# Attention in 64x64 array tiles, one block for output and next scores, the state summed in SBUF, and four PSUM banks for the MLP

## The chip, the cores and the metric

One core of one Trainium2 chip runs the program. The metric is the device time of an execution in microseconds (us); smaller is better. A run counts as slow when it is over 1.5% above the fastest of its kernel. Engines: PE is TensorE (PEld its weight loads), DVE is VectorE, ACT is ScalarE, POOL is GpSimd.

## The reference

A causal linear attention (4 batches, 8 heads, 768 positions, head size 64, a decay per head) feeds an MLP over 3072 tokens.

```python
intra = einsum('bhij,bhjd->bhid', einsum('bhic,bhjc->bhij', qb, kb) * Dmask, vb)   # per block of 64 positions
inter = einsum('bhid,bhde->bhie', qb * lam_pow, kv_state)
kv_state = lam_block * kv_state + einsum('bhsd,bhse->bhde', kb_dec, vb)
...
h = x @ w_in                     # x: 3072 x 512, w_in: 512 x 2048
s = sin(alpha * h)
g = h + s * s / (alpha + 1e-9)
out = g @ w_out                  # 2048 x 512
```

## The kernel before

The kernel works in 24 attention steps of 128 positions and in six MLP chunks of 512 tokens. A helper records every instruction, and a list scheduler in the program then fixes one static order for each engine; TensorE's order is the order of recording. Each engine works through its order as it stands, so an instruction that waits holds up those behind it.

An **A-group** is one slice of the first MLP half: four matmuls into one PSUM bank, a sine on ScalarE, a square on GpSimd (some on VectorE or ScalarE), and a **combine** on VectorE, which reads the bank a second time and so gives it back. A **B-group** is four matmuls of an output tile; after the last of four, ScalarE copies the tile out. An attention step is: **preparation** (k and q are scaled, v is cast), transposes of q and k, scores, the **mask** on VectorE (the causal mask times the scores, from PSUM into SBUF), output, and state.

```python
NPS = 5                                     # PSUM banks of the MLP
def next_bank():
    i = nm_at[0] % NPS
    nm_at[0] += 1
    return i

def att_S(s):                               # scores, then the mask
    ...
    for jp in range(HP):
        for h in range(2):
            rows = slice(64 * h, 64 * h + 64)
            last = e.matmul(A_ps[:, 4 * h + jp, :], qkT[j][rows, 4 + jp, :], qkT[j][rows, jp, :])
    ...
    rec("DVE", lambda e: e.tensor_tensor(S_m[j][:, :, :], A_ps[:, :, :], mask_b, ALU.mult), 1.25, ...)

def att_O(s, bank=None):                    # inter + intra, x copy, state in PSUM, two casts on ScalarE
    ...

def grp_A(c, m):
    i = next_bank()
    ...                                     # 4 matmuls -> m_ps[i]; sine on ACT -> t16
    if (c in (0, NCH - 1) and m % 4 == 3) or (c == 1 and m % 8 == 3):
        sq_eng, sq_dur = "DVE", 0.57
    elif c == 1 and m % 8 == 7:
        sq_eng, sq_dur = "ACT", 0.65
    else:
        sq_eng, sq_dur = "POOL", 1.05
    ...                                     # square -> u16; combine on DVE reads u16 and m_ps[i] -> gT

prep_next(4, fast=True)                     # at the end of A0: q of step 4 on DVE (fast), k on POOL
...
for m in range(NM):                         # A1: the first half of chunk 1, with steps 8 to 11
    op = grp_A(1, m)
    if m % 4 == 0:
        prep_next(9 + m // 4, soft=[op])
    attend(8, m, 4, 1, 3, 0)                # scores of the step at m % 4 == 1;
                                            # output, then the next step's transposes, at m % 4 == 3
    if m % 4 == 3:
        prep_v(9 + m // 4, soft=[P.ops[-1]])
```

The transposes write into the same PSUM pair `A_ps` that holds the scores until the mask has read them.

I name the stages by what runs: start (steps 0 to 3), A0 (first half of chunk 0), B0 (second half, with steps 4 to 7), A1 (first half of chunk 1, with steps 8 to 11), the mixed loop (second half of chunk c and first half of chunk c+1, with steps 12 to 23, then without attention), and the tail (second half of the last chunk).

Of the kernel before, what the change touches and what calls it, by code (L numbers as in the profile page):

```python
# [14 lines left out]
class Op:  # L15
    __slots__ = ("eng", "fn", "deps", "dur", "idx", "sem_after", "slot", "kslot",
                 "pos", "users", "start", "end", "nbytes", "clock", "prio", "signal", "soft", "soft_users")

    def __init__(self, eng, fn, dur, idx):
        self.eng, self.fn, self.dur, self.idx = eng, fn, dur, idx  # L20
        self.deps = set()
        self.soft = ()
        self.slot = None
        self.kslot = 0
        self.signal = False
        self.prio = idx


class Program:
# [110 lines left out]
    def emit(self, nc, sem):  # L140
# [9 lines left out]
        for op in order:  # L150
            k = known[op.eng]
            need = {}
            for d in op.deps:
                if d.slot is not None:
                    key, val = ("dma", d.slot), d.kslot
                else:
                    if d.eng == op.eng and op.slot is None and d.eng == "PE":
                        continue
                    key, val = d.eng, d.pos
                if k.get(key, 0) >= val:  # L160
                    continue
                if key not in need or need[key][0] < val:
                    need[key] = (val, d)
# [44 lines left out]
def bass_lightning_attn__then__act_snake_kernel(  # L208
# [24 lines left out]
    NPS = 5  # L233
# [5 lines left out]
    with es:  # L239
# [17 lines left out]
        Zs = ring("Zs", 2, [128, HP, 128], BF16)  # L257
# [26 lines left out]
        Z_ps = es.enter_context(nc.psum_tensor("Z_ps", [128, HP, D], F32))  # L284
# [11 lines left out]
        def next_bank():  # L296
            i = nm_at[0] % NPS
            nm_at[0] += 1
            return i
# [13 lines left out]
        def consts():  # L313
# [26 lines left out]
            for i in range(2):  # L340
                rec("DVE", lambda e, i=i: e.memset(Zs[i][:, :, :], 0.0), 0.3, writes=[f"Zs.{i}"])
# [3 lines left out]
        def alpha_ops():  # L345
            rec("ACT", lambda e: e.dma_start(alpha_r[:, :], moe_alpha.rearrange("(m p) -> m p", p=128)), 0,
                writes=["alpha_r"], slot="alpha", nbytes=8192)
            rec("PE", lambda e: e.transpose(Z_ps[:, 0, 0:NM], alpha_r[:, :], identf[0:NM, 0:NM]), 0.3,
                reads=["alpha_r", "identf"], writes=["Z"])
            rec("ACT", lambda e: e.copy(alpha_sb[:, :], Z_ps[:, 0, 0:NM]), 0.2, reads=["Z"], writes=["alpha"])  # L350
# [17 lines left out]
        def prep(s, fast=False, soft=()):  # L368
            n, r, c = s % NB, s % RL, s % RC
            Lq_b = bass.AP(Lq, n * H, [[NB * H, 128], [1, H], [0, D]])  # L370
            Lk_b = bass.AP(Lk, n * H, [[NB * H, 128], [1, H], [0, D]])
            done = rec("POOL", lambda e: e.tensor_tensor(k2[c][:, :, :], k32[r][:, :, :], Lk_b, ALU.mult), 1.05,
                       reads=[f"k32.{r}", "Lk"], writes=[f"k2.{c}"], soft=soft)
            rec("DVE" if fast else "POOL", lambda e: e.tensor_tensor(q2[c][:, :, :], q32[r][:, :, :], Lq_b, ALU.mult),
# [10 lines left out]
        def att_T(s, bank=None):  # L385
            c, j = s % RC, s % 2
            if bank is None:
                dst = bass.AP(A_ps, 0, [[1024, 128], [1, 512]]).bitcast(BF16).rearrange("p (a b) -> p a b", b=128)
                key = "S0"
# [4 lines left out]
            def pe(e):  # L394
                for jp in range(HP):
                    last = e.transpose(dst[:, jp, :], q2[c][:, 2 * jp:2 * jp + 2, :], ident[:, :])  # L396
                for jp in range(HP):
                    last = e.transpose(dst[:, 4 + jp, :], k2[c][:, 2 * jp:2 * jp + 2, :], ident[:, :])  # L398
                return last
            rec("PE", pe, 0.75, reads=[f"q2.{c}", f"k2.{c}", "ident"], writes=[key])  # L400
            rec("DVE", lambda e: e.tensor_copy(qkT[j][:, :, :], dst), 0.7, reads=[key], writes=[f"qkT.{j}"])  # L401

        def att_S(s):
            j = s % 2

            def pe(e):
                for jp in range(HP):
                    for h in range(2):
                        rows = slice(64 * h, 64 * h + 64)
                        last = e.matmul(A_ps[:, 4 * h + jp, :], qkT[j][rows, 4 + jp, :], qkT[j][rows, jp, :])  # L410
                return last
            rec("PE", pe, 0.6, reads=[f"qkT.{j}"], writes=["S0", "S1"])
            mask_b = bass.AP(mask, 0, [[128, 128], [0, 8], [1, 128]])
            rec("DVE", lambda e: e.tensor_tensor(S_m[j][:, :, :], A_ps[:, :, :], mask_b, ALU.mult), 1.25,  # L414
                reads=["S0", "S1", "mask"], writes=[f"S_m.{j}"])
            last_mask[0] = P.ops[-1]

        def att_O(s, bank=None):
            n, c, j = s % NB, s % RC, s % 2
            if bank is None:  # L420
                dst, key = A_ps[:, 4:8, :], "S1"
            else:
                dst = m_ps[bank][:, :].rearrange("p (a b) -> p a b", b=128)
                key = f"m.{bank}"
            has_state = n > 0

            def pe(e):
                if has_state:
                    for jp in range(HP):
                        e.matmul(dst[:, jp, :], Zs[(s - 1) % 2][:, jp, :], qkT[j][:, jp, :],  # L430
                                 start=(jp == 0), stop=False, skip_group_check=True)
                for jp in range(HP):
                    for h in range(2):
                        last = e.matmul(  # L434
                            dst[64 * h:64 * h + 64, jp, :], v2[c][:, 2 * jp + h, :], S_m[j][:, 4 * h + jp, :],
                            start=(not has_state and jp == 0), stop=(jp == HP - 1), skip_group_check=True)
                return last
            rec("PE", pe, 0.9,
                reads=[f"qkT.{j}", f"v2.{c}", f"S_m.{j}"] + ([f"Zs.{(s - 1) % 2}"] if has_state else []),
                writes=[key])  # L440
            ch, col = s // 4, 128 * (s % 4)
            x = ch % NX
            rec("ACT", lambda e: e.copy(xT[x][:, :, col:col + 128], dst), 0.62, reads=[key],  # L443
                writes=[f"x.{x}.{s % 4}"])
            if n < NB - 1:
                def pz(e):
                    for jp in range(HP):
                        for h in range(2):
                            last = e.matmul(
                                Z_ps[64 * h:64 * h + 64, jp, :], k2[c][:, 2 * jp + h, :], v2[c][:, 2 * jp + h, :],  # L450
                                start=(n == 0 and jp == 0), stop=(n == NB - 2 and jp == HP - 1),
                                skip_group_check=True)
                    return last
                rec("PE", pz, 0.3, reads=[f"k2.{c}", f"v2.{c}"], writes=["Z"])
                for h in range(2):
                    rows, cols = slice(64 * h, 64 * h + 64), slice(64 * h, 64 * h + 64)
                    rec("ACT", lambda e, rows=rows, cols=cols: e.copy(  # L457
                        Zs[j][rows, :, cols], Z_ps[rows, :, :]), 0.4, reads=["Z"], writes=[f"Zs.{j}"])
# [54 lines left out]
        def warm(n):  # L513
            def pe(e):
                for _ in range(n):
                    last = e.matmul(m_ps[2][:, :], ident[:, :], zeros[:, :])
                return last
            rec("PE", pe, 0.3 * n, reads=["ident", "zeros"], writes=["m.2"])
# [9 lines left out]
        W2_A, LD_A, W2_B, LD_B, LD_A1 = (7, 13), (10, 15), (2, 6), (3, 7, 11, 15), (3,)  # L528

# [11 lines left out]
        def attend(base, i, per, at_S, at_O, ahead, fast=False):  # L541
            s = base + i // per
            if s >= NSTEP:
                return
            if i % per == at_S:
                att_S(s)
                if ahead == 1:
                    prep_next(s + 1, fast, soft=[last_mask[0]])
            elif i % per == at_O:
                att_O(s)  # L550
                if ahead == 1:
                    prep_v(s + 1, soft=[P.ops[-1]])
                if s + 1 < NSTEP:
                    att_T(s + 1)
                if ahead == 2:
                    prep_next(s + 2, fast, soft=[last_mask[0]])
                    if s + 2 < NSTEP:
                        prep_v(s + 2, soft=[last_mask[0]])

        prep(0, fast=True)  # L560
        att_T(0, bank=3)
        for s in range(4):
# [5 lines left out]
            att_S(s)  # L568
            warm(2)
            if s < 3:  # L570
                att_T(s + 1, bank=3 if s % 2 else 4)
            warm(1)
            att_O(s, bank=s % 2)
# [12 lines left out]
        banks = [next_bank() for _ in range(4)]  # L586
        for m4 in range(4):
            for s4 in range(4):
                op = grp_B(0, s4, m4, banks[s4])
# [8 lines left out]
                if i in S_B:  # L598
                    s = 4 + S_B.index(i)
                    att_S(s)  # L600
                    prep_next(s + 1, fast=True, soft=[last_mask[0]])
                if i in O_B:
                    s = 4 + O_B.index(i)
                    att_O(s)
                    prep_v(s + 1, soft=[P.ops[-1]])
                    att_T(s + 1)
        for m in range(NM):
# [4 lines left out]
            if m % 4 == 0:  # L612
                prep_next(9 + m // 4, soft=[op])
            attend(8, m, 4, 1, 3, 0)
            if m % 4 == 3:
                prep_v(9 + m // 4, soft=[P.ops[-1]])
        prep_next(13, soft=[last_mask[0]])
        prep_v(13, soft=[last_mask[0]])
        for c in range(1, NCH):
            for i in range(NM):  # L620
                if i % 4 == 0:
                    bank = next_bank()
                grp_B(c, i // 4, i % 4, bank)
                if c + 1 < NCH:
                    attend(4 * (c + 2), 2 * i, 8, 2, 6, 2)
                    grp_A(c + 1, i)
                    attend(4 * (c + 2), 2 * i + 1, 8, 2, 6, 2)
# [34 lines left out]
```

## Time and profile before

The time was 234.58 us (median of 3 runs, 233.88 to 235.54), the profiled span 232.7 us. The stages below run from the first matmul of one to the first of the next.

| stage | start | A0 | B0 | A1 | mixed loop | tail |
|---|---|---|---|---|---|---|
| us | 22.51 | 15.82 | 25.64 | 21.84 | 129.82 | 17.10 |

The first two lines are the page's totals and the granted TensorE clock in 40 slices of the span (tenths, 9 is full).

```profile
PE 211.0 (91%) x1571; PEld 105.4 (45%) x1598; DVE 128.4 (55%) x169; ACT 123.2 (53%) x217; POOL 134.1 (58%) x141
...
PEclk9999999999999999999999999999999999999999
```

TensorE is the bound at 91% and no slice loses its clock. Where it isn't the bound is told by stages. The next view gives busy time of each engine in A0, A1, a stretch of the mixed loop and the tail.

```profile
core 0: us, PE busy (x) PEld busy (x) DVE busy (x) ACT busy (x) POOL busy (x), PEclk, DMA share, GB/s
22.50:38.30 15.80, 14.07 (x63) 6.07 (x65) 12.37 (x17) 11.10 (x18) 12.73 (x13) 1.00 1.18 208
...
64.00:85.80 21.80, 20.16 (x196) 11.03 (x201) 17.38 (x24) 18.00 (x34) 18.71 (x19) 1.00 1.21 236
85.80:187.20 101.40, 100.64 (x772) 50.70 (x783) 56.50 (x72) 58.56 (x103) 69.50 (x69) 1.00 0.41 92
...
215.60:232.70 17.10, 13.98 (x64) 6.17 (x64) 1.92 (x3) 3.03 (x5) 0.29 (x1) 1.00 0.20 77
```

In the mixed loop TensorE is busy 100.64 of 101.40 us, so only less work for TensorE helps there. In A1 all four engines are busy over 17 of 21.8 us: TensorE has hardly any waits, but nobody has much room.

One attention step of the mixed loop, as TensorE's timeline shows it (start, length, what, operation, out<-in, count):

```profile
122.81 0.40 PE L410 MATMUL A_ps<-qkT 64*128 64x128 bf16 x8
...
126.60 0.39 PE L430 MATMUL A_ps<-qkT,Zs 128*128 128x128 bf16 x4
126.92 0.41 PE L434 MATMUL A_ps<-S_m,v_1 128*64 128x128 bf16 x8
127.17 0.29 PE L449 MATMUL Z_ps<-v_1,k_1 128*64 128x64 bf16 x8
127.39 0.40 PE L396 MATMUL A_ps<-ident,q_2 128*128 128x128 bf16 x4
...
131.39 0.40 PE L410 MATMUL A_ps<-qkT 64*128 64x128 bf16 x8
```

From scores to scores a step takes 131.39 - 122.81 = 8.58 us. "64*128" and "128*64" are the shapes in which the array is used; it changes four times per step.

```profile
66.25 1.22 DVE L414 TENSOR_TENSOR S_m<-A_ps,mask 128x1024 bf16<-128x1024 f32 x1 [2.07 <-PE A_ps L410]
```

### The profile page before, as it was taken

How to read it: one execution, taken by the hardware profiler on the slowest of the kernel's cores; microseconds unless marked ns; L12 is line 12 of the kernel's file. 1: busy time of each engine (PE TensorE's matmuls, PEld its weight loads, DVE VectorE, ACT ScalarE, POOL GpSimd, SP SyncE). 2: the span in 40 equal slices, each digit the busy share in tenths (PEclk: the TensorE clock that was granted, in tenths of full speed). 3: DMA queues.
4: the chain of work that ended last, by engine and by line, in shares of the span. 5: the costliest groups of instructions: out<-in, count | busy, mean ns of one | idle time of the engine just before them, and what ended most of it. 6: DMA issues, size and time to landing. Idle time of an engine off the chain costs nothing.

```text
span 232.7 us, 3924 instructions
## 1 busy us (share of the span) xinstructions
PE 211.0 (91%) x1571; PEld 105.4 (45%) x1598; DVE 128.4 (55%) x169; ACT 123.2 (53%) x217; POOL 134.1 (58%) x141
## 2 busy tenths in 40 slices
PE   0687988697999989999999999999999999999994
PEld 0354433244455544455455455455455444444441
DVE  1664599745668876645636645546556535545300
ACT  4345774032787885655655655575465454454221
POOL 3253789340569897669568568758754554454100
PEclk9999999999999999999999999999999999999999
DMA  6999999999999999999670110111011011101112
GB/s 142 219 182 159 206 195 206 216 207 202 250 294 203 226 215 218 249 223 219 139 180 1 48 45 9 40 45 43 5 45 46 2 45 45 45 3 45 64 71 90
DMA packets 82752, 29.61 MB, mean 127 GB/s; under 512 B 75552, under 2 KB 79664, under 8 KB 82736
## 3 DMA queue, kind: packets, MB, share of 16 engines
q1 hardware_dynamic: 74880, 18.88, 42.7%
q0 software_dynamic: 4224, 4.19, 11.4%
q10 hardware_dynamic: 3632, 6.31, 7.4%
q8 instruction: 12, 0.20, 0.4%
q14 instruction: 4, 0.03, 0.0%
HBM read 27.28 MB, written 6.29 MB: 144 GB/s over the span
## 4 chain that ended last, share of the span: by engine, by line
PE 73%; DVE 8%; DMA 5%; SPq 4%; ACT 3%; issue 2%; POOL 2%; ACTq 0%; POOLq 0%
PE m_ps L498 33%; PE m_ps L470 28%; SPq L310 4%; DVE gT L488 3%; DMA w<-in_moe_w_out_dram 3%; PE A_ps L410 3%; DVE S_m L414 3%; PE A_ps L434 2%; DMA q_3<-in_q_dram 2%; PE A_ps L396 2%; PE A_ps L398 1%; POOL u_1 L486 1%; PE A_ps L430 1%; POOL u_0 L486 1%; ACT xT L443 1%
## 5 line engine op out<-in xcount | busy, mean ns | idle before, releaser
L498 PE MATMUL m_ps<-w,gT 128*128 128x512 bf16 x377 | 94.0, 380 | 2.7 <-DVE gT L488 1.3
L470 PE MATMUL m_ps<-xT,w 128*128 128x512 bf16 x366 | 92.3, 380 | 3.8 <-DVE gT L488 1.7
L498 PEld LDWEIGHTS m_ps<-w,gT 128*128 128x128 bf16 x384 | 36.6, 98 | 46.6 <-DVE gT L488 1.7
L470 PEld LDWEIGHTS m_ps<-xT,w 128*128 128x128 bf16 x384 | 35.2, 98 | 43.0 <-DVE gT L488 3.1
L486 POOL TENSOR_TENSOR u_0<-t_0 128x512 bf16<-128x512 bf16 x24 | 25.1, 1047 | 23.1 <-ACT t_0 L474 23.1
L414 DVE TENSOR_TENSOR S_m<-A_ps,mask 128x1024 bf16<-128x1024 f32 x24 | 29.4, 1223 | 11.7 <-PE A_ps L410 11.0
L488 DVE SCALAR_TENSOR_TENSOR gT<-u_1,r_sb,m_ps 128x512 bf16<-128x512 bf16 x24 | 17.9, 746 | 23.3 <-POOL u_1 L486 23.3
L488 DVE SCALAR_TENSOR_TENSOR gT<-u_3,r_sb,m_ps 128x512 bf16<-128x512 bf16 x24 | 17.9, 744 | 20.7 <-POOL u_3 L486 19.9
L486 POOL TENSOR_TENSOR u_1<-t_1 128x512 bf16<-128x512 bf16 x24 | 24.9, 1038 | 5.1 <-ACT t_1 L474 5.0
L486 POOL TENSOR_TENSOR u_2<-t_2 128x512 bf16<-128x512 bf16 x24 | 24.9, 1039 | 5.1 <-ACT t_2 L474 5.0
L474 ACT ACTIVATE t_2<-m_ps,alpha_sb 128x512 bf16<-128x512 f32 x24 | 16.5, 687 | 19.4 <-PE m_ps L470 19.3
L474 ACT ACTIVATE t_1<-m_ps,alpha_sb 128x512 bf16<-128x512 f32 x24 | 16.5, 687 | 18.1 <-PE m_ps L470 18.1
L486 POOL TENSOR_TENSOR u_3<-t_3 128x512 bf16<-128x512 bf16 x12 | 12.5, 1039 | 23.0 <-ACT t_3 L474 23.0
L474 ACT ACTIVATE t_0<-m_ps,alpha_sb 128x512 bf16<-128x512 f32 x24 | 16.5, 687 | 15.3 <-PE m_ps L470 15.2
L488 DVE SCALAR_TENSOR_TENSOR gT<-u_0,r_sb,m_ps 128x512 bf16<-128x512 bf16 x24 | 17.8, 740 | 10.1 <-POOL u_0 L486 10.1
L488 DVE SCALAR_TENSOR_TENSOR gT<-u_2,r_sb,m_ps 128x512 bf16<-128x512 bf16 x24 | 17.9, 744 | 9.6 <-POOL u_2 L486 9.6
L443 ACT CAST xT<-A_ps 128x512 bf16<-128x512 f32 x20 | 11.6, 582 | 20.9 <-PE A_ps L434 15.4
L506 ACT COPY osb<-m_ps 128x512 f32<-128x512 f32 x24 | 14.1, 586 | 15.6 <-PE m_ps L498 15.5
L474 ACT ACTIVATE t_3<-m_ps,alpha_sb 128x512 bf16<-128x512 f32 x24 | 16.5, 687 | 4.0 <-PE m_ps L470 3.8
L401 DVE COPY qkT<-A_ps 128x1024 bf16<-128x1024 bf16 x20 | 13.7, 684 | 4.7 <-PE A_ps L398 4.7
L457 ACT CAST Zs<-Z_ps 64x256 bf16<-64x256 f32 x40 | 14.6, 366 | 0.6
L410 PE MATMUL A_ps<-qkT 64*128 64x128 bf16 x192 | 10.0, 226 | 2.0 <-DVE qkT L401 1.9
(173 smaller groups left out, 176.8 us busy)
## 6 DMA issues: line engine op xcount, KB each, us to landing
out_dram<-osb ACTq DMA_DIRECT2D x24, 256.0 KB, 2.0
w<-in_moe_w_in_dram POOLq DMA_DIRECT2D x4, 512.0 KB, 8.0
w<-in_moe_w_out_dram POOLq DMA_DIRECT2D x4, 512.0 KB, 6.8
k_0<-in_k_dram SPq DMA_DIRECT2D x4, 256.0 KB, 4.4
q_0<-in_q_dram SPq DMA_DIRECT2D x4, 256.0 KB, 5.1
v_0<-in_v_dram SPq DMA_DIRECT2D x4, 256.0 KB, 5.4
k_1<-in_k_dram SPq DMA_DIRECT2D x4, 256.0 KB, 5.5
q_1<-in_q_dram SPq DMA_DIRECT2D x4, 256.0 KB, 5.8
```

The lines of the kernel that those rows point to most:

```text
L310: rec_load(lambda e, a=a, d=dst[r]: e.dma_start(d[:, :, :], a), [f"{nme}32.{r}"], f"{nme}{r}", 330000, after)
L401: rec("DVE", lambda e: e.tensor_copy(qkT[j][:, :, :], dst), 0.7, reads=[key], writes=[f"qkT.{j}"])
L410: last = e.matmul(A_ps[:, 4 * h + jp, :], qkT[j][rows, 4 + jp, :], qkT[j][rows, jp, :])
L414: rec("DVE", lambda e: e.tensor_tensor(S_m[j][:, :, :], A_ps[:, :, :], mask_b, ALU.mult), 1.25, reads=["S0", "S1", "mask"], writes=[f"S_m. ...
L443: rec("ACT", lambda e: e.copy(xT[x][:, :, col:col + 128], dst), 0.62, reads=[key], writes=[f"x.{x}.{s % 4}"])
L457: rec("ACT", lambda e, rows=rows, cols=cols: e.copy(Zs[j][rows, :, cols], Z_ps[rows, :, :]), 0.4, reads=["Z"], writes=[f"Zs.{j}"])
L470: last = e.matmul(m_ps[i][:, :], w1[:, kc, 128 * m:128 * (m + 1)], xT[x][:, kc, :], start=(kc == 0), stop=(kc == NKC - 1))
L474: rec("ACT", lambda e: e.activation(t16[tt][:, :], m_ps[i][:, :], ACTF.Sin, scale=alpha_sb[:, m:m + 1]), 0.7, reads=[f"m.{i}", "alpha"], w ...
L486: return e.tensor_tensor(u16[tt][:, :], t16[tt][:, :], t16[tt][:, :], ALU.mult)
L488: rec("DVE", lambda e: e.scalar_tensor_tensor(out=gT[g][:, m, :], in0=u16[tt][:, :], scalar=r_sb[:, m:m + 1], in1=m_ps[i][:, :], op0=ALU.m ...
L498: last = e.matmul(m_ps[bank][:, :], gT[g][:, m, 128 * s4:128 * (s4 + 1)], w2[:, m, :], start=(m == 0), stop=(m == NM - 1))
L506: rec("ACT", lambda e: e.copy(osb[o][:, :], m_ps[bank][:, :]), 0.6, reads=[f"m.{bank}"], writes=[f"o.{o}"])
```

## The change

The intent is to give TensorE less to do per attention step. All attention products use 64x64 tiles of the array, four of which run at the same time. One block holds the first half of the output of step o, the scores of the next step s, and the second half of the output, so the array changes shape twice instead of four times per step. The state is added up in SBUF by VectorE (`Zacc`) and cast by GpSimd, instead of staying in PSUM and being cast twice by ScalarE. The output now takes a PSUM pair of its own, so the MLP has four banks, and bank 0 of these is kept for B-groups: A-groups rotate over three.

```diff
-    NPS = 5
+    NPS = 4
@@
         def next_bank():
-            i = nm_at[0] % NPS
+            i = 1 + nm_at[0] % (NPS - 1)
@@
-        def att_S(s):
-        def att_O(s, bank=None):
+        def mm_S(e, s, h, ch):
+            r, a, j = h // 4, h % 4, s % 2
+            return e.matmul(A_ps[half(ch), h, :], qkT[j][half(r), 4 + a, half(ch)], qkT[j][half(r), a, :])
+        ...                                              # mm_intra, mm_inter, mm_Z: 64x64 tiles as well
+        def att(o, s):
+            ...
+                fence = rec("PE", first, 0.3, reads=reads, writes=["O"])
+            if s is not None:
+                rec("PE", scores, 0.25, reads=[f"qkT.{s % 2}"], writes=["S"])
+            if o is not None:
+                op = rec("PE", second, 0.3, reads=reads, writes=["O"])
+                op.fence = fence
+            if has_Z:
+                ...  op = rec("DVE", lambda e: e.tensor_tensor(acc, z, acc, ALU.add), 0.4, ...)   # Zacc
+            ...      rec("ACT", lambda e: e.copy(xo, O_ps[:, :, 0:2, :]), 0.62, ..., after=after)
+            ...      rec("POOL", lambda e: e.tensor_copy(Zs[o % 2][:, :, :], Zacc[:, :, :]), 0.35, ...)
+            ...      # then the mask of s on DVE
@@
+        SEC_A1, PREP_A1 = (1, 4, 8, 12, 15), (0, 3, 6, 9, 12)
@@
-                op = grp_B(0, s4, m4, banks[s4])
+                op = grp_B(0, s4, m4, s4)
@@                                                       # A1
-            if m % 4 == 0:
-                prep_next(9 + m // 4, soft=[op])
-            attend(8, m, 4, 1, 3, 0)
-            if m % 4 == 3:
-                prep_v(9 + m // 4, soft=[P.ops[-1]])
-        prep_next(13, soft=[last_mask[0]])
-        prep_v(13, soft=[last_mask[0]])
+            if m in PREP_A1:
+                prep_next(9 + PREP_A1.index(m), soft=[op])
+            if m in PREP_A1:
+                prep_v(9 + PREP_A1.index(m), soft=[op])
+            if m in SEC_A1:
+                s = 8 + SEC_A1.index(m)
+                att(s - 1 if s > 8 else None, s)
+                att_T(s + 1)
@@                                                       # mixed loop
-                grp_B(c, i // 4, i % 4, bank)
+                grp_B(c, i // 4, i % 4, 0)
...                                                      # att at i % 4 == 2, transposes at i % 4 == 3
```

The `fence` makes the second half of the output wait for the end of the first, both on TensorE; between TensorE's other instructions the program leaves such waits out.

## The prediction

> **What bounds it now.** Span 232.7 us, TensorE busy 91%, clock 1.00 (page). By stretches (busy table): start to 22.5 us; A0 (first MLP half of chunk 0) 22.5-38.3; B0 (second half, with attention) to 64.0; A1 to 85.8; the mixed loop to 187.2, where TensorE is busy 100.6 of 101.4 us; chunk 4/5 without attention to 215.6; tail. In the mixed loop the timeline gives 8.58 us per attention step: 32 MLP matmuls at 216 ns (6.91) plus 1.67 for attention. Of that 1.67 about 1.29 is streaming and four times ~95 ns is lost where the array shape changes (149 ns between starts instead of 55; 310 instead of 216). The Trainium skill, "TensorEngine Tiling (Array Packing)", Key Properties, says a mode change drains TensorE; the trace agrees. In A1 POOL is busy 18.7 of 21.8 us.
>
> **Gain, on the critical path.** One 64x64 block holds output and next scores; transposes stay 128x128: two shape changes per step instead of four (-0.19 us). Tile pairs start 4 ns apart now, every 53 ns (N=128) or 27 (N=64); with four tiles I estimate first 0.22, scores 0.21, second 0.30, transposes 0.45, changes 0.19: 1.4 us against 1.67. The fence between the halves is covered by the scores in the loop, exposed (~0.2 us) in start and B0. I subtract ~0.1 us: transposes wait for the mask (1.22 us), now behind the state addition on DVE. Mixed loop: about -2.6 us, one score block of that being moved to A1.
>
> **Cost, also on the critical path.**
> - A-groups rotate over three banks only (bank 0 is kept for B). A bank is held 0.65 + 0.42 (last matmul to sine) + 0.69 sine + 0.08 + 1.04 square + 0.04 + 0.74 combine = 3.65 us, plus ~0.06 to return. Five banks: 0.74 us per group, hidden under 0.865. Three: 1.24. So A0 becomes bank-bound: 19.4 us instead of 15.8, and the q preparation on DVE (1.85 us), inside it, is no longer absorbed: about +5 us. B0's second group waits for A0's last bank (+1 us), but the w_out wait (1.0 us) vanishes.
> - Tail: all four last output tiles use bank 0. Each hand-over costs last matmul to copy 0.42 + 0.06 + copy 0.59 + 0.06 = 1.12 instead of 0.22 us; three times +2.7.
> - A1: POOL gets five preparations and three state copies (~0.5 us): about 21.5 us of work after the first square; +2.2 us.
> - Start: x copy behind the state addition, fence: +0.8 us.
> - ACT loses 40 state copies (14.6 us): free time, no gain.
>
> **Sum.** 0.8 + 5 + 0.5 + 2.2 - 2.6 + 2.7 = +8.6 us. Predicted 243 us, range 235 to 250. Faster by over 2%: 0.08; within 2%: 0.20; slower: 0.72.
>
> **What would show it.** A0's matmul starts in bursts of three groups per ~3.7 us, TensorE waiting for the DVE combine; A0 ≥ 19 us. Mixed period ~8.4 us, two ~95 ns losses per step, four tiles starting within ~12 ns. Three ~0.9 us waits on the output copy in the tail. A1 ~24 us, POOL near full. ACT busy ~-14 us.
>
> **What would make it wrong.** TensorE may not be fed 112 small instructions per block (the trace proves only ~32 ns per instruction over 128); then it is slower still. Four tiles might not run together. Or early losses are absorbed by waits I counted as fixed and attention shrinks below 1.2 us: then it is within 2%.

## More of the kernel before

The waits of TensorE, in total over the span (us, times, longest), are few:

```profile
PE A_ps L410 <- DVE qkT L401: 1.9, 3, 0.8
PE m_ps L470 <- DVE gT L488: 1.7, 2, 1.1
PE m_ps L498 <- DVE gT L488: 1.3, 2, 1.0
```

No wait for the mask before the transposes is among them. In A1 the mask (third line) runs while TensorE does two A-groups:

```profile
65.81 0.40 PE L410 MATMUL A_ps<-qkT 64*128 64x128 bf16 x8
...
68.66 0.40 PE L396 MATMUL A_ps<-ident,q_4 128*128 128x128 bf16 x4
```

## The result, and the profile after

The changed kernel took 256.56 us (median of 4 runs, 256.16 to 257.71) against 235.06 us (233.88 to 235.66) for the kernel before in the same rounds. The ratio is 1.093, with a 95% interval of 1.0885 to 1.0974. Ratios here are the mean time of one kernel's fast runs over the mean of the other's in the same rounds, so not quite the ratio of the medians that I quote.

| stage (us) | start | A0 | B0 | A1 | mixed loop | tail | span |
|---|---|---|---|---|---|---|---|
| before | 22.51 | 15.82 | 25.64 | 21.84 | 129.82 | 17.10 | 232.75 |
| after | 24.04 | 21.55 | 25.40 | 37.04 | 126.55 | 19.76 | 254.34 |
| difference | +1.5 | +5.7 | -0.2 | +15.2 | -3.3 | +2.7 | +21.6 |
| predicted | +0.8 | +5 | +0.5 | +2.2 | -2.6 | +2.7 | +8.6 |

Five of six terms are near, and their errors cancel. A1's error, 15.2 less 2.2, is the 13 us by which the sum was off.

The totals and the clock of the page after; the clock now falls in the slices of A1:

```profile
PE 211.1 (83%) x2193; PEld 103.3 (41%) x2222; DVE 133.0 (52%) x187; ACT 110.2 (43%) x177; POOL 141.8 (56%) x161
...
PEclk9999999999998697999999999999999999999999
```

The busy times by stretch, for A0, A1, the mixed loop with attention and the tail:

```profile
24.00:45.60 21.60, 15.29 (x63) 5.50 (x66) 11.93 (x17) 10.83 (x16) 13.67 (x14) 1.00 0.89 157
...
71.00:108.00 37.00, 24.13 (x324) 12.85 (x328) 21.43 (x30) 17.49 (x29) 24.85 (x27) 0.86 1.10 225
108.00:204.90 96.90, 94.86 (x1050) 48.06 (x1062) 57.13 (x79) 48.82 (x78) 69.01 (x75) 1.00 0.23 64
...
234.50:254.30 19.80, 14.54 (x64) 5.93 (x64) 1.92 (x3) 3.06 (x6) 0.33 (x1) 1.00 0.18 66
```

In A1 no engine is busy more than 24.85 of 37.0 us. No engine's throughput bounds it; the engines wait for each other in turn. TensorE's waits (total, times, longest) say on whom:

```profile
PE A_ps L398 <- DVE S_m L508: 10.0, 5, 4.0
PE m_ps L522 <- DVE gT L540: 8.5, 6, 2.6
...
PE m_ps L550 <- ACT osb L558: 2.1, 3, 0.7
```

The first line is new: the five transposes of A1 wait for the mask. The second is the A-groups' wait for a bank (6 times in A0 and A1), the third the tail. The worst mask wait, on TensorE's timeline:

```profile
77.82 0.39 PE L410 MATMUL A_ps<-qkT 64*64 64x128 bf16 x14
...
82.42 0.61 PE L398 MATMUL A_ps<-ident,q 128*128 128x128 bf16 x4 [3.95 <-DVE S_m L508]
82.82 0.63 PE L400 MATMUL A_ps<-ident,k 128*128 128x128 bf16 x4
83.67 5.28 PE L522 MATMUL m_ps<-xT,w 128*128 128x512 bf16 x15 [0.22 <-issue]
```

and on VectorE's, whose fixed order has a square, the state addition and three combines ahead of the mask:

```profile
78.13 0.79 DVE L538 TENSOR_TENSOR u<-t 128x512 bf16<-128x512 bf16 x1 [1.70 <-ACT t L526]
78.84 0.41 DVE L495 TENSOR_TENSOR Zacc<-O_ps,Zacc 128x256 f32<-128x256 f32 x1
79.18 2.05 DVE L540 SCALAR_TENSOR_TENSOR gT<-u,r_sb,m_ps 128x512 bf16<-128x512 bf16 x3
81.15 1.21 DVE L508 TENSOR_TENSOR S_m<-A_ps,mask 128x1024 bf16<-128x1024 f32 x1
```

ScalarE was late as well: its sines stood behind a v copy that waited 2.93 us for a load. That turned out to matter little for this wait (the run with later v copies below still has 3.69 us of it).

```profile
76.32 0.62 ACT L384 CAST v<-v 128x512 bf16<-128x512 f32 x1 [2.93 <-DMA v<-in_v_dram]
76.84 1.84 ACT L526 ACTIVATE t<-m_ps,alpha_sb 128x512 bf16<-128x512 f32 x3
```

The wait has a second cost. The fifteen matmuls at 83.67 take 5.28 us: at first they start some 428 ns apart instead of 216. Over A1 twelve pairs are so far apart, which lost 2.5 us (sum of their distances less 216 ns each). The Trainium skill, "TensorE: Matmul & The Clock Gate", Part 1: The HAM clock gate, says that the array's clock is halved after an idle window of about 3.4 us and that it takes about as long to come back; the trace agrees here in the halving after a wait of 3.95 us, while the way back took longer, about 5.1 us (from 82.42 to 87.49 us).

In the mixed loop and the tail the prediction's picture is there. From block to block a step now takes 129.68 - 121.33 = 8.35 us instead of 8.58:

```profile
121.33 0.24 PE L414 MATMUL O_ps<-S_m,v 64*64 64x128 bf16 x2
...
129.68 0.24 PE L419 MATMUL O_ps<-qkT,Zs 64*64 64x128 bf16 x2
```

A change of the array's shape costs about 93 ns (309 ns between starts where 216 is usual), and there are two per step, as predicted. The Trainium skill, "TensorEngine Tiling (Array Packing)", Key Properties, says that a mode change drains TensorE; the 93 ns fit that, without showing what they are spent on. In the tail each new output tile waits for the copy of the last:

```profile
238.94 3.63 PE L550 MATMUL m_ps<-w,gT 128*128 128x512 bf16 x16 [0.73 <-ACT osb L558]
243.30 3.63 PE L550 MATMUL m_ps<-w,gT 128*128 128x512 bf16 x16 [0.73 <-ACT osb L558]
247.61 3.63 PE L550 MATMUL m_ps<-w,gT 128*128 128x512 bf16 x16 [0.68 <-ACT osb L558]
```

### The profile page after: what moved, and what is told of

The parts are those of the page before. It is cut to its first block, busy times and chain, and to the rows that moved or that the text cites. A ratio compares the mean times of both kernels' runs of the same rounds, so it can differ in the third digit from the quotient of the medians.

```text
span 254.3 us, 5115 instructions
## 1 busy us (share of the span) xinstructions
PE 211.1 (83%) x2193; PEld 103.3 (41%) x2222; DVE 133.0 (52%) x187; ACT 110.2 (43%) x177; POOL 141.8 (56%) x161
## 4 chain that ended last, share of the span: by engine, by line
PE 62%; DMA 13%; DVE 8%; SPq 6%; ACT 5%; POOL 3%; issue 2%; ACTq 0%
PE m_ps L550 28%; PE m_ps L522 26%; SPq L312 6%; DMA w<-in_moe_w_in_dram 4%; DVE gT L540 4%; DMA v<-in_v_dram 3%; ACT t L526 3%; DMA w<-in_moe_w_out_dram 3%; PE O_ps L414 2%; DVE S_m L508 2%; DMA k<-in_k_dram 2%; PE A_ps L398 2%; DMA q<-in_q_dram 2%; POOL u L538 2%; PE A_ps L410 1%
## 5 line engine op out<-in xcount | busy, mean ns | idle before, releaser
L538 POOL TENSOR_TENSOR u<-t 128x512 bf16<-128x512 bf16 x84 | 86.8, 1041 | 57.2 <-ACT t L526 56.9
L540 DVE SCALAR_TENSOR_TENSOR gT<-u,r_sb,m_ps 128x512 bf16<-128x512 bf16 x96 | 70.4, 744 | 68.4 <-POOL u L538 66.5
L526 ACT ACTIVATE t<-m_ps,alpha_sb 128x512 bf16<-128x512 f32 x96 | 65.7, 687 | 75.8 <-PE m_ps L522 75.6
L374 POOL TENSOR_TENSOR k<-k,Lk 128x512 bf16<-128x512 f32 x24 | 25.3, 1055 | 10.6 <-DMA k<-in_k_dram 7.5
L501 ACT CAST xT<-O_ps 128x512 bf16<-128x512 f32 x24 | 14.0, 585 | 36.1 <-DVE Zacc L495 25.7
L384 ACT CAST v<-v 128x512 bf16<-128x512 f32 x24 | 14.7, 616 | 7.6 <-DMA v<-in_v_dram 7.6
L414 PE MATMUL O_ps<-S_m,v 64*64 64x128 bf16 (+1 forms) x384 | 15.4, 215 | 2.2 <-DVE S_m L508 1.6
L376 POOL TENSOR_TENSOR q<-q,Lq 128x512 bf16<-128x512 f32 x15 | 15.6, 1043 | 0.0
L419 PE MATMUL O_ps<-qkT,Zs 64*64 64x128 bf16 x160 | 14.1, 232 | 0.0
L410 PE MATMUL A_ps<-qkT 64*64 64x128 bf16 x384 | 10.7, 225 | 0.8 <-DVE qkT L403 0.8
L424 PE MATMUL O_ps<-v,k 64*64 64x64 bf16 x320 | 11.0, 196 | 0.0
```

Source lines behind the costliest of these rows:

```text
L374: done = rec("POOL", lambda e: e.tensor_tensor(k_out, k_in, Lk_b, ALU.mult), 1.05, reads=[f"k32.{r}", "Lk"], writes=[f"k2.{c}"], soft=soft)
L376: rec("DVE" if fast else "POOL", lambda e: e.tensor_tensor(q_out, q_in, Lq_b, ALU.mult), 0.6 if fast else 1.05, reads=[f"q32.{r}", "Lq"], ...
L384: rec("ACT", lambda e: e.copy(v2[c][:, :, :], v32[r][:, :, :]), 0.62, reads=[f"v32.{r}"], writes=[f"v2.{c}"], soft=soft)
L414: return e.matmul(O_ps[half(h % 2), g, a, i0:128], v2[c][half(r), h, :], S_m[j][half(r), h, i0:128], start=start, stop=True, skip_group_ch ...
L526: rec("ACT", lambda e: e.activation(t16[tt][:, :], m_ps[i][:, :], ACTF.Sin, scale=alpha_sb[:, m:m + 1]), 0.7, reads=[f"m.{i}", "alpha"], w ...
L538: return e.tensor_tensor(u16[tt][:, :], t16[tt][:, :], t16[tt][:, :], ALU.mult)
```

## The experiments

The theory after the result: A1 lost its time to **order and buffers**, not to load. Transposes that stand directly behind the scores in the same PSUM pair must wait for the mask; the mask stands in VectorE's fixed order behind combines which wait for squares, which wait for sines; and three banks leave TensorE no slack to cover it. The rival is the prediction's own reason, GpSimd's load by the fifth preparation and the state casts. A third suspect is the v copies' place on ScalarE.

All kernels gave correct results. Stage times are from each kernel's profiled run; ratios are to the kernel before in the same rounds. One profile's stage time is not exact: in stages that an edit left as in the changed kernel, the start took 24.0 to 25.7 us, A0 20.5 to 22.0 and A1 37.0 to 37.8. In the rounds of sections 1 and 3 and of two runs of section 4 (both changes in the kernel before; squares on ScalarE), many runs of the kernel before were slow (4 of 7, 5 of 11, 3 of 11), and the record gives the verdict "unclear" there; the ratios that I quote are still those of fast runs alone.

### 1. Single remedies in the changed kernel

**Transposes of A1 into the idle MLP bank 0** (so that they need not wait for the mask):

```diff
-                att_T(s + 1)
+                att_T(s + 1, bank=0 if m < 15 else None)
```

> The changed kernel with one edit: in A1 (the second chunk's first MLP half) the transposes that stand directly behind a score block go to MLP bank 0, which is idle there, instead of to the score banks that the mask still has to read (four of the five times). Theory W (transposes wait for the mask, and everything behind them): the waits of 1.6, 4.1, 2.5 and 1.1 us before the transposes vanish, the clock stays at 1.00 in A1, A1 falls from 37.0 to about 25 us and the time from 256.5 to about 245. Rival L (the copies of v, early in ScalarE's fixed order, wait for loads and hold up the sines): A1 falls by less than 4 us, the waits reappear at the next score or MLP group. Rival B (three MLP banks are too few): nothing, at most 1 us.

Measured: 248.16 us, ratio 1.0571 (1.0497 to 1.0645). A1 fell from 37.04 to 29.90 us (-7.1). The waits for the mask went from 10.0 to 1.6 us, and waits for combines, that is for banks, rose from 8.5 to 10.7. The order of the transposes is worth about half of A1's loss, and what it uncovers is the banks.

**v copies of A1 later** (behind the blocks instead of with the preparation):

```diff
-            if m in PREP_A1:
-                prep_v(9 + PREP_A1.index(m), soft=[op])
+            if m in V_A1:                                # (3, 7, 11, 14, 15)
+                prep_v(9 + V_A1.index(m), soft=[op])
```

> The changed kernel with one edit: in A1 the copies of v are recorded 3 to 4 MLP groups later, each still before the output block that needs it. Theory L: the 2.9 us wait of ScalarE for the load of v vanishes, with it the 4.1 us wait of TensorE and the throttled clock; A1 falls from 37.0 to about 27, the time to about 247. Theory W: the waits of the transposes for the mask stay, at 1.5 to 2.5 us each, five times; the 4.1 us one shrinks to that and the clock stays up; A1 falls by 3 to 5 us, time about 252. Theory B: nothing.

Measured: 254.14 us, ratio 1.0838 (1.0716 to 1.0959). A1 fell by 2.0 us to 35.07. The waits for the mask stayed (10.6 us, the longest 3.7). So the load that held up ScalarE is not the main cause: it made the longest wait 0.26 us longer. VectorE's order makes nearly all of it. In this run the state addition (0.42 us, which needs the end of the block), three combines (2.05) and the mask (1.22) follow each other without a gap from 78.68 to 82.21 us, which is 3.53 of the 3.69 us that the transposes wait:

```profile
78.68 0.42 DVE L495 TENSOR_TENSOR Zacc<-O_ps,Zacc 128x256 f32<-128x256 f32 x1 [0.52 <-PE O_ps L424]
79.02 2.05 DVE L540 SCALAR_TENSOR_TENSOR gT<-u,r_sb,m_ps 128x512 bf16<-128x512 bf16 x3
80.99 1.22 DVE L508 TENSOR_TENSOR S_m<-A_ps,mask 128x1024 bf16<-128x1024 f32 x1
```

**Four banks instead of three in A0 and A1** (bank 0 included, as B-groups don't need it then):

```diff
-            i = 1 + nm_at[0] % (NPS - 1)
+            i = nm_at[0] % NPS if chunk[0] < 2 else 1 + nm_at[0] % (NPS - 1)
```

> The changed kernel with one edit: in A0 and A1 the MLP groups rotate over all four MLP banks instead of three (bank 0 is idle there). All theories, for A0: 3.7 us hold over four banks is 0.93 us per group, so A0 falls from 21.6 to about 17 us. For A1: theory B says that it falls by 8 us or more (time about 243); theories W and L say by less than 2 us (time about 251).

Measured: 251.4 us, ratio 1.0699 (1.0571 to 1.0828). A0 fell by 2.8 us to 18.72, A1 by 5.6 to 31.40, between the two readings (8 or more; under 2); B0 gave 1.7 back. The mask waits stayed at 8.6 us.

**Tail over four banks**:

```diff
-                grp_B(c, i // 4, i % 4, 0)
+                grp_B(c, i // 4, i % 4, 0 if c + 1 < NCH else i // 4)
```

> The changed kernel with one edit: the four last output tiles of chunk 5 use banks 0 to 3 instead of all bank 0. The three waits of 0.9 us on the output copy vanish: 2.7 us less, about 253.8 us. Were the tail limited elsewhere (gelu-like combine of the last group, output DMA), the gain would be under 1 us.

Measured: 254.14 us, ratio 1.0825 (1.0718 to 1.0931). The tail fell from 19.76 to 17.10 us, exactly the tail of before. This is the term of the prediction that was right in cause and size.

### 2. Remedies together

**A1 put in order**: transposes two A-groups behind the scores (the last ones, of step 13, in the mixed loop), v copies late, four banks in A1.

```diff
-        SEC_A1, PREP_A1 = (1, 4, 8, 12, 15), (0, 3, 6, 9, 12)
+        SEC_A1, T_A1, PREP_A1 = (0, 4, 8, 12, 15), (2, 6, 10, 14), (0, 3, 6, 9, 12)
@@
                 att(s - 1 if s > 8 else None, s)
-                att_T(s + 1)
+            if m in T_A1:
+                att_T(9 + T_A1.index(m))
...                      # v copies and banks as above; att_T(13) in the mixed loop
```

> The changed kernel with A1 alone edited, three edits together: transposes two MLP groups behind the scores that they overwrite (the last of them in the mixed loop), copies of v later, and four MLP banks in A1. If the order in A1 and its banks are the whole of its loss: no wait of TensorE for the mask over 0.7 us in A1, clock 1.00, A1 from 37.0 to about 24 us, time about 244. Rival (GpSimd's own load, five preparations and three state copies beside twelve squares, bounds A1): GpSimd busy over 90% of A1 and A1 no shorter than 28 us, time about 248.

Measured: 244.09 us median; ratio of the fast runs 1.0362 (1.0299 to 1.0424). The profiled run was odd: 1200.95 us, with every matmul some 1280 ns from the next at a recorded clock of 1.0. It counts as slow, I have no explanation for it, and its profile is not used. The three timed runs were 243.06 to 244.31.

**A0 over five banks** (the four and one half of the output pair, which is idle in A0):

```diff
+            i = nm_at[0] % 5 if chunk[0] == 0 else 1 + nm_at[0] % (NPS - 1)
+            ps = m_ps[i][:, :] if i < NPS else bass.AP(O_ps, 0, [[1024, 128], [1, 512]])
...                      # the sine and the combine read ps, too
```

> The changed kernel with A0 alone edited: its MLP groups rotate over five banks as before the change (the four MLP banks and half of the output pair, idle in A0). If three banks are the whole of A0's loss: A0 from 21.6 to 16 to 17 us, time about 252. Rival (the preparation of q on VectorE, or the loads, hold A0 up whatever the banks, as the four-bank run, 18.7 us, might hint): A0 stays near 18.7.

Measured: 256.49 us, ratio 1.088 (1.0806 to 1.0954): nothing to tell from the changed kernel. The profile fell into a slow run (259.38 us), so I read only its order of events. The first ten groups ran without a wait for a bank; then TensorE waited 3.00 us for a combine (the changed kernel has a wait of 2.55 us near there). And my edit had a flaw: the last group of A0 landed on bank 0, which B0's first tile needs, which cost another wait of 3.20 us. The expected gain went into these two waits.

**All remedies**: the last two and the tail's four banks.

> The changed kernel with the edits of A0 (five banks), A1 (later transposes and copies, four banks) and tail (a bank per tile) together. If the three losses are independent and all that there is beside the start: start 24, A0 17, B0 25.5, A1 24, mixed loop with the rest of the MLP 127, tail 17.1, in all a span of 234.6 and a time of about 236.5, within 1% of the kernel before. If they hide each other (a gain in one stage given back in the next, loads that are not there), 240 or more.

Measured: 242.01 us (6 runs), ratio 1.0296 (1.0249 to 1.0342). A1 is 22.33 us: the joint block, the state sum and the preparations are all still there, and 14.7 of the 15.2 us are gone (2.0 of them came back in the mixed loop, which now holds the transposes of step 13 and begins with a wait for a bank). The next view, in the columns of the busy times above, shows what is left in A1:

```profile
71.90:94.23 22.33, 19.45 (x316) 10.72 (x320) 18.66 (x27) 16.01 (x27) 22.00 (x25) 1.00 1.04 227
```

GpSimd is now busy 22.00 of 22.33 us. So the prediction's count of GpSimd's work was a fair floor for A1; it was not what made 37 us of it.

The total is not the 236.5 us that I expected of independent losses, but falls under the other reading, 240 or more. A0 is still 21.48 us, of which 2.63 is the wait that my flaw in the rotation makes. The reason for the other wait, 3.00 us for a combine, stands on VectorE's timeline

```profile
34.42 3.83 DVE L376 TENSOR_TENSOR q<-q,Lq 128x512 bf16<-128x512 f32 x1
38.17 0.73 DVE L543 SCALAR_TENSOR_TENSOR gT<-u,r_sb,m_ps 128x512 bf16<-128x512 bf16 x1
```

and on GpSimd's at the same time:

```profile
33.66 3.04 POOL L541 TENSOR_TENSOR u<-t 128x512 bf16<-128x512 bf16 x3
36.66 1.03 POOL L374 TENSOR_TENSOR k<-k,Lk 128x512 bf16<-128x512 f32 x1
```

The q preparation, which mostly takes 0.63 to 0.70 us on VectorE in these kernels, took 3.83 us. It ended at 38.25, which is 0.56 us after GpSimd's unbroken run of four operations ended at 37.69. In the kernel before, the same operation took 1.85 us and ended at 34.33, 0.57 us after GpSimd's run had ended at 33.76. The Trainium skill, "SBUF — State Buffer", section "SBUF: two separate sides", says that a VectorE operation with two SBUF inputs and a GpSimd operation that reads SBUF exclude each other for a whole instruction. The 3.83 us fit that, though they span several GpSimd instructions (see the last section); and the combine, with one input in PSUM, took 0.73 to 0.75 us throughout A0.

**All remedies, and the x copy ahead of the state addition in step 3 of the start**:

```diff
-            att(s, None)
+            att(s, None, x_first=s == 3)
```

> The same with one more edit: in the last step of the start the output is copied to x before the state is added up, not after. If the state addition on VectorE delays A0's start: 0.4 us less than the run beside it, all of it in the start. If the start is bound by the loads, nothing.

Measured: 241.86 us, ratio 1.028 (1.0237 to 1.0323), against 1.0296 without it. No difference that these runs can tell; the +1.5 us of the start are not explained by this order.

### 3. What was left of A0, and the mirror in the kernel before

**Rotation of A0 begun on the fifth bank**, so that its last group does not land on bank 0:

```diff
-            i = nm_at[0] % 5 if chunk[0] == 0
+            i = (nm_at[0] + 4) % 5 if chunk[0] == 0
```

> The combination of remedies (transposes two groups later, v copies later, four banks in A1, five in A0, tail over four banks), with the only difference that A0's rotation starts at the half of O_ps, so that its last group lands on O_ps and bank 0, which B0's first tile needs, is free earlier. If the 3.0 us gap at the start of B0 was only this artefact, A0 falls from 21.5 to 18.5 us and the total from 242.0 to about 239 (ratio about 1.017). Rival: the gap only moves (the second tile waits for bank 1 or 2, or the combines end as late as before): A0 stays within 0.5 us of 21.5.

Measured: 239.77 us, ratio 1.0198 (1.0147 to 1.0248). A0 18.68 us, as expected; B0's first wait was the flaw of my edit.

**The q preparation of step 4 on GpSimd**, on top of that:

```diff
-        prep_next(4, fast=True)
+        prep_next(4)
```

> As the run before, and step 4's q preparation at the end of A0 is moved from VectorE (where it took 3.83 us, ending 0.6 us after GpSimd's run of back-to-back squares ended) to GpSimd. Theory that VectorE is starved by GpSimd on an operation with two SBUF inputs: no VectorE operation above 1.6 us is left in A0, the 3.4 us gap of TensorE in A0 goes, A0 is 16 to 17.5 us, total 236 to 238 (ratio 1.005 to 1.015). Rival, that A0 is bound by the amount of work on GpSimd: the 1.05 us more on GpSimd makes A0 no shorter than in the run before.

Measured: 237.95 us, ratio 1.0122 (1.0078 to 1.0167). The total was met, A0 was not: it stayed at 19.47 us (1.6 of which its first two groups lost at half clock). The slow operation had only moved. VectorE's next operation with two SBUF inputs, a square, took 3.56 us

```profile
37.73 3.56 DVE L541 TENSOR_TENSOR u<-t 128x512 bf16<-128x512 bf16 x1
```

while GpSimd ran without a gap until 41.00:

```profile
34.98 3.04 POOL L541 TENSOR_TENSOR u<-t 128x512 bf16<-128x512 bf16 x3
37.98 1.03 POOL L374 TENSOR_TENSOR k<-k,Lk 128x512 bf16<-128x512 f32 x1
38.98 2.02 POOL L541 TENSOR_TENSOR u<-t 128x512 bf16<-128x512 bf16 x2
```

The square ended at 41.29. B0 was shorter by 2.8 us, mostly because a 1.5 us wait for a load of w_out, and the half clock of the matmuls soon after it, did not occur in this run; I claim no cause for that.

**The kernel before, with A1's transposes directly behind the scores**:

```diff
             if i % per == at_S:
                 att_S(s)
+                if ahead == 0:
+                    att_T(s + 1)
```

(and no longer behind the output in A1)

> The kernel before, with one thing of the change: in A1 the transposes of the next step stand directly behind the scores, in the same PSUM pair, instead of two MLP groups later. Theory (placement makes waits for the mask): from the trace of before each of four transposes would then wait 1.2 to 1.4 us for the mask (mask 1.22 us, begun when the scores end), so A1 grows by 3 to 5 us from 25.64/21.84 (B0/A1) to A1 25 to 27 us, total about 239 (ratio 1.015 to 1.02); with five banks and no state addition VectorE is less far behind than in the changed kernel, so the 4 us wait does not appear. Rival (GpSimd throughput sets A1, placement is free): A1 stays 21.8 +- 0.5, ratio 1.00.

Measured: 243.27 us, ratio 1.034 (1.027 to 1.041). A1 grew by 4.4 us to 26.28, inside the expected 3 to 5. Each of the four transposes waits 1.41 us, three of them for the mask (its 1.23 us and the way to and from it), the last for a preparation; two of them:

```profile
72.50 0.38 PE L396 MATMUL A_ps<-ident,q 128*128 128x128 bf16 x4 [1.41 <-DVE S_m L414]
79.10 0.38 PE L396 MATMUL A_ps<-ident,q 128*128 128x128 bf16 x4 [1.41 <-DVE S_m L414]
```

The total grew by more, since B0 was 4.9 us longer in the profiled run: a load of w_out landed later (TensorE waited 2.37 us instead of 0.99) and eight matmuls then started 428 ns apart. TensorE's order is the same as before up to A1, so this is not the edit's place to act; I don't count it, and can't say why the load was late.

**The kernel before, with three banks in A0 and A1**:

```diff
-            i = nm_at[0] % NPS
+            i = 1 + nm_at[0] % 3 if n == 3 else nm_at[0] % NPS      # n is 3 in A0 and A1
...                      # B0's tiles on banks 0 to 3, then the rotation starts anew
```

> The kernel before, with its first MLP half rotating over three PSUM banks in A0 and A1 instead of five (all else as before; the mixed loop keeps five). If three banks alone make A0's loss: A0 15.8 to 19.5-21 us, with TensorE waiting for the combine. A1: the bank period 1.24 us per group times 16 is 19.8 us plus attention, so if banks alone explain A1's loss, A1 becomes 30 us or more; if placement is needed too, A1 grows by 2 to 5 us only. Total 242 to 246 in the second case (ratio 1.03 to 1.045).

Measured: 247.83 us, ratio 1.0546 (1.0485 to 1.0607). A0 grew by 7.2 us to 23.03, A1 by 5.6 to 27.46, and the total is above the expected 242 to 246. Banks alone do not make A1's 37 us.

### 4. Both together, and the starved operations

**The kernel before, with both** (edits of the last two):

> The kernel before, with both single changes: A1's transposes directly behind the scores, and three banks for A0 and A1. Alone they lengthened A1 by 4.4 and 5.6 us. If they add, A1 is 31.9 us (21.84 + 4.4 + 5.6); if they feed each other (TensorE idle longer, half clock, VectorE's order), it is 33 us or more; if the one wait hides in the other, 28 to 30. The changed kernel has 37.0. Ratio to before about 1.08 to 1.09.

Measured: 248.87 us, ratio 1.0602 (1.0521 to 1.0684). A1 29.65 us, +7.8 where the parts were +4.4 and +5.6: the waits partly cover each other. The mask starts at once here, so that each wait is again 1.41 us, and no matmul in A1 ran at half clock:

```profile
81.37 0.38 PE L396 MATMUL A_ps<-ident,q 128*128 128x128 bf16 x4 [1.41 <-DVE S_m L414]
88.31 0.38 PE L396 MATMUL A_ps<-ident,q 128*128 128x128 bf16 x4 [1.41 <-DVE S_m L414]
```

**A0's four VectorE squares on ScalarE** (on top of q on GpSimd):

```diff
-            if (c in (0, NCH - 1) and m % 4 == 3) or (c == 1 and m % 8 == 3):
+            if (c == NCH - 1 and m % 4 == 3) or (c == 1 and m % 8 == 3):
                 sq_eng, sq_dur = "DVE", 0.57
-            elif c == 1 and m % 8 == 7:
+            elif (c == 1 and m % 8 == 7) or (c == 0 and m % 4 == 3):
                 sq_eng, sq_dur = "ACT", 0.65
```

> As the last combination (q preparation on GpSimd), and A0's four squares that VectorE did (m % 4 == 3) are on ScalarE. In the last run the long VectorE operation of A0 was no longer the q preparation but a square of 3.56 us, which TensorE then waited 3.0 us for. Theory (every VectorE operation with two SBUF inputs is starved while GpSimd runs back to back): with none left in A0 apart from the combines (one input in PSUM), no VectorE instruction of A0 is over 0.8 us and A0 falls from 19.5 to 15.5 to 16.5 us, total 234 to 235.5 (ratio 0.995 to 1.003). Rival (GpSimd's own queue delays A0): the longest wait of TensorE in A0 stays about 3 us and A0 above 18 us, now ended by GpSimd's squares.

Measured: 237.92 us, ratio 1.0099 (1.002 to 1.0179). A0 fell to 16.34 us, again with 1.6 lost at half clock in its first two groups, and had no wait of TensorE for a combine left. So A0 was held by starved VectorE operations and not by the amount of GpSimd's work, which this run does not reduce. But the total did not fall as expected: the transposes of step 4 now waited 1.73 us for the q preparation on GpSimd, which is about half of what B0 grew by (26.88 us against 23.73).

**The first group of chunk 2 on bank 1**, which A1 gave up longest ago:

```diff
+        nm_at[0] = 0
         for c in range(1, NCH):
```

> As the run before, and the first MLP half of the mixed loop starts its rotation on bank 1, which A1 gave up longest ago, instead of bank 2. The 1.6 us wait for a combine at the first group of chunk 2 should fall by 0.7 to 0.9 us, nothing else should change: total 0.5 to 1 us below the run before, 233.5 to 235 (ratio 0.99 to 1.00): at best level with the kernel before.

Measured: 236.65 us, ratio 1.0052 (0.9997 to 1.0107). The wait fell from 1.58 to 0.83 us and the mixed loop by 0.9 us; the total came out above the expected range. A0 was 14.78 us without the half clock. This is the best version of the change that I found, and it does not beat the kernel before.

**The kernel before, with A0's squares on ScalarE and step 4's q preparation on GpSimd** (edits as above):

> The kernel before, with the four squares of A0 on ScalarE instead of VectorE and step 4's q preparation on GpSimd. In its trace VectorE's squares took up to 1.5 us and the q preparation 1.85 us in A0, and TensorE had waits of 1.15, 0.52 and 1.02 us for combines there and at the start of B0. If they are the same starvation, A0 and the first wait of B0 shorten by 1 to 2 us together and the total by about that (ratio 0.993 to 0.998); if the step-4 transposes then wait for GpSimd instead, nothing is gained (1.00).

Measured: 233.65 us (233.15 to 234.77, 6 fast runs), ratio 0.9938 (0.9886 to 0.999). A0 went from 15.82 to 14.82 us, although the transposes of step 4 wait 1.63 us here too. It has the lowest time, by 0.6%. The same repair is in the last kernel above, which took 236.65 us in the same rounds, so like for like the repaired change is 1.0052 / 0.9938 = 1.011 times the repaired kernel before (a quotient; no interval was recorded for it).

### 5. The rest of A1

**The kernel before, with both, and A1's preparations as in the change** (five, with v copies at once):

```diff
-            if m % 4 == 0:
-                prep_next(9 + m // 4, soft=[op])
+            if m in (0, 3, 6, 9, 12):
+                prep_next(9 + m // 3, soft=[op])
+                prep_v(9 + m // 3, soft=[op])
...                      # the later v copies and step 13's preparation behind A1 are cut
```

> The kernel before with both single changes (29.65 us in A1) and, as a third part of the change, A1's preparations as the changed kernel has them: five instead of four inside A1 (at groups 0, 3, 6, 9, 12), the v copies on ScalarE directly with them. If the preparations and early v copies are what lifts 29.65 to the changed kernel's 37.0, A1 is 35 us or more. If the rest belongs to the state sum and the joint block of output and next scores, which this kernel doesn't have, A1 is 29 to 32 us.

Measured: 253.4 to 254.46 us in three slow runs and 249.4 in the only fast one; no ratio is given. Inconclusive. The profile is of a slow run (A1 33.81 us), and the fast run is within the range of the kernel without this part (248.36 to 251.57 us), so the preparations' cost can't be told.

**The changed kernel, with the fifth preparation moved out of A1** and its transposes into the mixed loop:

```diff
-        SEC_A1, PREP_A1 = (1, 4, 8, 12, 15), (0, 3, 6, 9, 12)
+        SEC_A1, PREP_A1 = (1, 4, 8, 12, 15), (0, 3, 6, 9)
...                      # step 13 is prepared behind A1; att_T(13) in the mixed loop
```

> The changed kernel with only A1's fifth preparation (step 13: k and q on GpSimd, v on ScalarE) moved behind A1 and its transposes into the mixed loop, as the kernel before has them. This tests the prediction's own term, that GpSimd's load by the fifth preparation sets A1's growth: if so A1 falls by 2 to 3 us from 37.0. If the order and the banks set it, A1 falls by 1.1 to 1.9 us at most (the 1.6 us wait of the last transposes and their 0.45 us leave A1, and some comes back in the mixed loop): total 255 to 256 (ratio 1.085 to 1.09).

Measured: 256.5 us, ratio 1.0878 (1.0772 to 1.0984), the time of the changed kernel. A1 fell by 1.6 us to 35.40 and the mixed loop grew by 1.3. The longest wait for the mask, 4.07 us, stood where it had stood, though GpSimd was busy 20.8 us of A1 instead of 24.9. The two expectations lie close together (2 to 3 us; 1.1 to 1.9), and 1.6 alone would not decide. But with the total unmoved here, and all five preparations inside the 22.33 us of "All remedies", GpSimd's load is refuted as the reason for A1's +15.2 us.

## Why the prediction was wrong

**The step that failed** is this term: "A1: POOL gets five preparations and three state copies (~0.5 us): about 21.5 us of work after the first square; +2.2 us." It measured +15.2 us. The term took A1 to be bound by the busiest engine and added up that engine's work. The runs show that no engine was the bound: POOL was busy 24.85 of 37.0 us, and taking the fifth preparation away changed nothing in the total. As a floor the count was fair (22.33 us with GpSimd busy 22.00 once the waits were gone); the term left out the waits and what follows from them, the other 14.7 us. What took its place is order and buffers:

- Transposes directly behind the scores. Moved off that PSUM pair in the changed kernel: -7.1 us. Put there in the kernel before: +4.4 us.
- Three banks. A fourth in the changed kernel: -5.6 us. Three in the kernel before: +5.6 us.
- v copies with the preparations: -2.0 us when late.
- All three put right at once: -14.7 us in A1, with the last transposes moved into the mixed loop, which grew by 2.0 us.

The single removals add up to 14.7 us as well, but the additions don't: both in the kernel before give 7.8 us, and the changed kernel's A1 is 7.4 us longer than that. With the order, the banks and the v copies put right, the joint block and the state sum cost A1 only 0.5 us (22.33 against 21.84), so the 7.4 us are no separate cost of theirs but arise where they meet the bad order: VectorE's addition and combines in front of the mask made one wait of 3.95 us where it is 1.41 when the mask comes first, and matmuls at half clock lost 2.5 us. Which part of it makes how much is open.

I had the warning in hand and priced it at 0.1 us: "transposes wait for the mask (1.22 us), now behind the state addition on DVE". I took it from the mixed loop, where a group of matmuls stands between, and did not check it in A1, where the change puts nothing between.

The other terms:

- **A0, +5 predicted, +5.7 measured.** The cause was half right. Three banks lengthen A0 (+7.2 us in the kernel before), but the q preparation's time was not the fixed 1.85 us that I took from the trace: it depends on how long GpSimd runs without a gap. With five banks back and that left as it was, A0 gained 2.9 us (18.68, once the rotation no longer ended on bank 0), no more than with four banks (18.72); with two-input operations off VectorE as well it was 14.8 us, shorter than before.
- **Tail, +2.7 predicted, +2.7 measured.** Right, and shown by the run that took it away.
- **Mixed loop, -2.6 predicted, -3.3 measured.** Right in mechanism and nearly in size. My fear that small instructions might not be fed fast enough did not come true.
- **Start, +0.8 predicted, +1.5 measured.** Right in direction. The same start took up to 25.7 us in other profiles, so its size is not settled. The one order that I tested for it changed nothing; its cause was argued and is not shown.
- **ACT loses 14.6 us: no gain.** Its busy time fell by 13.0 us (123.2 to 110.2), and nothing came of it.

Was there a gain in the change at all? In its best version the mixed loop is 1.9 us shorter than before (127.88 against 129.82), while start (+1.7), B0 (+1.4) and A1 (+0.6) give back more, and A0's -1.0 is not the change's but the repair's, which works in the kernel before too.

## What to carry to other kernels

When a change moves an instruction in a static order, read for each buffer that it writes who must have read it, and how far ahead of it that reader stands on its own engine: a wait costs what stands in front of the reader, not only the reader's own time (here 3.69 to 3.95 us for a mask of 1.22). Cost this stage by stage, and don't carry a wait's price from a stage that covers it to one that doesn't. And a duration in a trace is not a constant where two engines share something: see what the other engine was doing at the time before you reuse the number.

## What the Trainium skill lacked or had wrong

- "SBUF — State Buffer", "SBUF: two separate sides": it says that whichever of the two operations starts first has the ports for its whole instruction, and the other blocks. It does not say that a VectorE operation can be held through several GpSimd instructions that start after it. Here one recorded as starting at 34.42 us ended at 38.25, through three GpSimd instructions that started after it, and took 3.83 us instead of 0.68; in three kernels such an operation ended 0.3 to 0.6 us after GpSimd's unbroken run.
- "TensorE: Matmul & The Clock Gate", Part 1: it gives an idle window of about 3.4 us for the halved clock. Here matmuls ran some 428 ns apart after a wait of 3.95 us, but also after waits of 2.52 us (at 97.83 us in the changed kernel) and 2.37 us (in the kernel before with the transposes moved), and within 2 us after one of only 1.52 us (at 56.67 us in the run with A0's rotation begun on the fifth bank), and not after one of 2.65 us (with the v copies late). The page notes that the window runs freely, and further on that frequent short idle times can do it too, either of which could be why; no run here shows it.
- "TensorEngine Tiling (Array Packing)", Key Properties: it says that a mode change drains TensorE but gives no cost. In these traces a change costs about 93 ns (309 ns between starts instead of 216).
